# Row sums of the softmax taken in four 64x64 blocks of TensorE instead of four 128x32 strips, and a first quad whose keys are transposed unnormalised, in a fused attention and SoLU block

## The chip, the cores and the metric

The kernel runs on one core of a Trainium2 chip. The metric is the device time of one execution in microseconds (us). Three executions of the kernel before took 782.05, 782.74 and 783.13 us, so the median is 782.74 us. Engines have the names of the profile: PE is TensorE (PEld its weight loads), DVE is VectorE, ACT is ScalarE, POOL is GpSimd, and SP is SyncE, which issues most of the DMAs; SPq, ACTq and POOLq are the queues of instructions of those engines.

## What is computed

```python
# attention: q, k, v are (8, 12, 448, 64) float32
rmsnorm(x, g) = x / sqrt(mean(x * x, axis=-1) + 1e-6) * g
q_n, k_n = rmsnorm(q, g_q), rmsnorm(k, g_k)
scores = q_n @ k_n.T / sqrt(64)
attn = exp(scores - max(scores))
attn = attn / (sum(attn) + 1e-9)
x = (attn @ v) laid out as (3584, 768)
# SoLU block: w_in (768, 1024), w_out (1024, 768), float64 as given
h = x @ w_in
u = h * softmax(h)
out = layernorm(u) * g_ln @ w_out
```

The kernel does not subtract the maximum of the scores: the normalised rows and the gains bound them, and a second, general path takes over where they do not. That path does not run on these inputs.

## The kernel before

The 96 heads are worked on in 24 groups of four, called quads; a quad is two pairs of heads, `i` = 0, 1 numbers the pair and `h` = 0, 1 the head in it. Everything on PE is float32, and each matmul of the program stands in the trace as two MATMUL records, since float32 is done in two parts.

**A quad of the steady state (quads 1 to 23).** The 448 keys of a head are 7 blocks of 64. For each block, `both_scores` (line 870, matmul in L879) multiplies keys by queries of all four heads: four matmuls of 64 rows by 64 columns by 448 queries, each in another quarter of the PE array, which therefore run at the same time. I call four such matmuls a set; a set is 8 records. ACT takes the exponentials of the set's 128x896 result in one instruction (L839). `both_values` (line 884, L891) multiplies the exponentials by v, again one set for each block. So a quad is 14 sets. The score tiles stand in PSUM buffers with the tag `t`, of which there are three.

**The sums of the softmax.** DVE adds some of a quad's seven tiles of exponentials together first (`add_pair`, `add_to`), so that 4 tiles are left for each of quads 1 and 2, and 3 for each of quads 3 to 23. What is left is called the terms. `sums` (line 941, L951) adds each term's partitions on PE with a matrix of ones, for one quad, then two, then three quads at a time (`sums_at`, line 1458: after quads 2, 5, 8 and so on to 23; quad 0 has its own). A term takes four matmuls: all 128 partitions, 32 columns of ones, and a quarter of the 896 columns, 224, each, in four column strips of the array. ACT copies the result (`keep_sums`, line 957, at most two copies), and a DMA stores it for a later stage that divides by it.

```python
sm[g : g + 32, j % 2, j // 2 * S // 2 : (j // 2 + 1) * S // 2], ones[:, w], e[:, h, t * S // 2 : (t + 1) * S // 2],
```

**Quad 0, the start.** Nothing can be prefetched for it, so it has functions of its own. `load_rows` brings q and k of its two pairs in rows (112 partitions of four rows), through SP's queue (q) and ACT's (k). For pair 0, DVE and ACT square q and k, DVE sums the squares (`sum_rows`, L783), ACT starts the reciprocal root (`rsqrt_seed`, L713 and L714) and DVE improves it (`rsqrt_step`, L720 to L723), DVE multiplies (`normalise_rows`, L802), PE transposes (L809), and ACT copies the transposed q and k out of PSUM (`take_rows`, L817 and L819). The gains of q and k come as one column through POOL, DVE, PE and ACT (`gain_column`). Then come three score tiles of pair 0 (L849), one tile of the last 64 keys of all four heads (`scores_last`, L862), three of pair 1, the values (L925, and L936 with 128 rows by 64 columns, two matmuls at a time), and the sums of 5 terms: three of pair 0's tiles were added by DVE (`add`, L910) and POOL (`add_more`, L914). Before all this PE runs five matmuls on zeros (`warm_up`, L793).

The order of all instructions is written out by hand (`tc.manual_schedule`, from line 1492); each engine takes its own in that order. After the attention come the products with w_in (L1103) and w_out (L1329) on PE.

Of the kernel before, what the change touches and what calls it, by code (L numbers as in the profile page):

```python
# [366 lines left out]
def fast_path(  # L367
# [58 lines left out]
    ones = work.tile([P, 3, 32], FP32, tag="ones", name="ones", bufs=1)  # L426
# [22 lines left out]
    def setup():  # L449
        nc.gpsimd.memset(mhalf, -0.5)  # L450
        nc.gpsimd.memset(seven, 7.0)
        nc.gpsimd.memset(eps, 1e-6)


        for i, x in enumerate((-1.9375, -1.00390625, -(0.1249 ** 2))):
            nc.gpsimd.memset(limits[:, i : i + 1], x)


        nc.gpsimd.memset(ones, 0.0)
        for i in range(2):  # L460
            c = slice(16 * i, 16 * i + 16)
            nc.gpsimd.memset(ones[:, i, c], 1.0)
            nc.gpsimd.memset(ones[i * D : (i + 1) * D, 2, c], 1.0)
        make_identity(nc, ident)
# [17 lines left out]
    def gain_column():  # L482
# [10 lines left out]
        pg = ps_t.tile([P, KF], FP32, tag="t", name="pg")[:, 0:1]  # L493
        nc.tensor.transpose(pg, gg[:, 2:4].rearrange("o h d -> o (h d)"), ident[0:1, 0:1])
        nc.scalar.copy(gcol[:, KF : KF + 1], pg)
# [181 lines left out]
    def squares_half(n, s, vector):  # L677
# [4 lines left out]
        if vector:  # L682
            nc.vector.tensor_tensor(y, x, x, OP.mult)
        else:
            nc.scalar.activation(y, x, AF.Square)
# [61 lines left out]
    def qk_transpose(n):  # L747
        d = st[n]
        turned(n)
        nc.vector.transpose(d["qkT"].rearrange("p s t -> p (s t)"), d["qkn"].rearrange("p b d -> p (b d)"))  # L750
# [8 lines left out]
    def load_rows(n, queues):  # L759
        b, hp = divmod(n, NP)  # L760
        d = st[n] = {}
        d["qk"] = xs.tile([P, 2, 2, 4, D], FP32, tag="x", name="x")[0:R]
        for s, src in enumerate((q, k)):
            for h in range(2):
                queues[2 * s + h].dma_start(
                    d["qk"][:, s, h], src[b, 4 * (hp // 2) + hp % 2 + 2 * h].rearrange("(p j) d -> p j d", p=R)
                )

    def square_rows(n, s, engine):
        d = st[n]  # L770
        if s == 0:
            d["sq"] = xs.tile([P, 2, 2, 4, D], FP32, tag="x", name="xsq")[0:R]
        x, y = d["qk"][:, s], d["sq"][:, s]
        if engine is nc.scalar:
            nc.scalar.activation(y, x, AF.Square)
        else:
            engine.tensor_tensor(y, x, x, OP.mult)

    def sum_rows(n, s):
        d = st[n]  # L780
        if s == 0:
            d["ss"] = work.tile([P, 4 * NB], FP32, tag="ss", name="ss", bufs=2)[0:R, 0:16]
        nc.vector.tensor_reduce(  # L783
            d["ss"][:, s * 8 : s * 8 + 8], d["sq"][:, s].rearrange("p h j d -> p (h j) d"), AX, OP.add
        )

    def warm_up():

        w = work.tile([P, 2, S], FP32, tag="el", name="warm", bufs=3)[:, 0]
        nc.vector.memset(w, 0.0)  # L790
        o = ps_t.tile([P, 2, 512], FP32, tag="o", name="pt", bufs=1)[:, 0, 0:S]
        for _ in range(5):
# [5 lines left out]
    def normalise_rows(n, s):  # L798
        d = st[n]
        y = d["y"][:, s * 8 : s * 8 + 8].rearrange("p (h j) -> p h j ()", h=2).to_broadcast([R, 2, 4, D])  # L800
        o = flat(d["sq"][:, s]).rearrange("p (j h d) -> p h j d", h=2, d=D)
        nc.vector.tensor_tensor(o, d["qk"][:, s], y, OP.mult)  # L802

    def transpose_rows(n, s):
        d = st[n]
        pt = ps_t.tile([P, 2, 512], FP32, tag="o" if n and s == 0 else "t", name="pt", bufs=1 if n and s == 0 else 3)
        d["pt", s] = pt[:, 0, 0:S]
        for j in range(4):
            nc.tensor.transpose(  # L809
                d["pt", s].rearrange("p (r j) -> p j r", j=4)[:, j], flat(d["sq"][:, s])[:, j * P : (j + 1) * P], ident[0:R, 0:R]  # L810
            )

    def take_rows(n, s):
        d = st[n]
        if s == 0:
            turned(n)
# [1100 lines left out]
```

## Time and profile before

| what | value |
| --- | --- |
| three executions | 782.05, 782.74, 783.13 us |
| the profiled execution: its time / its span (first to last instruction) | 781.84 us / 780.0 us |
| granted TensorE clock, mean | 0.998 |
| PE busy | 771.0 us, 5262 instructions |
| DVE, ACT, POOL busy | 603.6, 508.9, 487.3 us |
| DMA moved | 134.27 MB, mean 172 GB/s |

The profile is one execution. Its page gives each engine's busy time, the span in 40 slices, the chain of work that ended last, and the costliest groups of instructions; other views of the same trace list the waits of an engine, the chain in order of time, and the instructions of an engine in order of time. In such a row the first number is the start, the second the time taken, both in us; a group of instructions is merged into one row with its count (x8 is 8 records), and brackets hold the idle time ahead of it and what ended it. Matmul records are pipelined, so the time of one record (0.54 us for 448 columns) is longer than what it costs in a stream; the cost is read from the distance between starts, which the chain's rows give.

### The profile page before, as it was taken

What the parts mean: (1) busy time and instruction counts of PE and PEld (TensorE: products, weight loads), DVE (VectorE), ACT (ScalarE), POOL (GpSimd) and SP (SyncE); (2) the same over time, 40 slices, a digit from 0 to 9 for tenths busy, and PEclk for the clock granted to TensorE, in tenths of its full rate; (3) what the DMA queues carried; (4) which work ended last, traced back from release to release, by engine and by line L of the source; (5) the groups of instructions that cost most, each with busy time, mean ns of one, the idle gap of its engine ahead of it and who ended that gap; (6) DMA issues with size and microseconds to landing.
All of it is one profiled execution on the core that took longest, in us unless ns stands there. A gap on an engine that the chain in (4) does not pass through costs nothing.

```text
span 780.0 us, 15087 instructions
## 1 busy us (share of the span) xinstructions
PE 771.0 (99%) x5262; PEld 478.3 (61%) x5262; DVE 603.6 (77%) x1064; ACT 508.9 (65%) x833; POOL 487.3 (62%) x635
## 2 busy tenths in 40 slices
PE   8999999999999999999999999999999999999997
PEld 4444445445454444444444444444899999999996
DVE  6878999999999983687777667685797695776844
ACT  6778898888989862787777656655626445464510
POOL 2565444455464552455687688888898787777862
PEclk9999999999999999999999999999999999999999
DMA  9999999999999367588887777773757647456312
GB/s 164 173 188 192 194 198 176 200 209 187 186 203 172 91 171 165 130 196 182 195 203 169 161 150 165 163 182 69 224 154 240 207 145 256 144 188 242 104 62 87
DMA packets 279818, 134.27 MB, mean 172 GB/s; under 512 B 190324, under 2 KB 264884, under 8 KB 279732
## 3 DMA queue, kind: packets, MB, share of 16 engines
q1 hardware_dynamic: 265892, 123.31, 70.4%
q10 hardware_dynamic: 13840, 9.90, 4.4%
q8 instruction: 44, 0.72, 0.4%
q14 instruction: 42, 0.34, 0.1%
HBM read 96.12 MB, written 37.04 MB: 171 GB/s over the span
## 4 chain that ended last, share of the span: by engine, by line
PE 94%; SPq 3%; DMA 1%; DVE 0%; POOL 0%; ACT 0%; issue 0%; POOLq 0%; ACTq 0%
PE A L1329 16%; PE o L891 15%; PE s L879 15%; PE A L1103 14%; PE B L1103 9%; PE B L1329 8%; PE D L1103 5%; PE C L1103 5%; PE C L1329 4%; PE sm L951 4%; SPq L647 2%; DMA qk<-in_k_dram 0%; DMA gg<-in_g_q_dram 0%; DVE part L696 0%; POOL ss L706 0%
## 5 line engine op out<-in xcount | busy, mean ns | idle before, releaser
L879 PE MATMUL s<-qkT 64*64 64x448 f32 x1288 | 139.3, 540 | 0.3 <-ACT qkT L745 0.2
L839 ACT ACTIVATE E<-s 128x896 f32<-128x896 f32 x144 | 124.5, 920 | 20.5 <-PE s L879 19.7
L729 POOL TENSOR_TENSOR qkn<-qk,ny 128x896 f32<-128x896 f32 x45 | 77.2, 1736 | 72.9 <-DVE ny L723 33.5
L891 PE MATMUL o<-E,v 64*64 64x448 f32 x1104 | 120.4, 536 | 0.0
L879 PEld LDWEIGHTS s<-qkT 64*64 64x64 f32 x1288 | 66.1, 191 | 60.0 <-issue 38.8
L1329 PE MATMUL A<-w_out,sums 128*128 128x192 f32 x392 | 79.8, 326 | 0.0
L1329 PE MATMUL B<-w_out,sums 128*128 128x192 f32 x392 | 79.8, 326 | 0.0
L891 PEld LDWEIGHTS o<-E,v 64*64 64x64 f32 x1104 | 42.4, 133 | 56.2 <-issue 49.0
L1103 PE MATMUL A<-w_in,xg 128*128 128x512 f32 x168 | 76.8, 593 | 0.0
L1103 PE MATMUL B<-w_in,xsum 128*128 128x512 f32 x168 | 76.7, 592 | 0.0
L1329 PEld LDWEIGHTS B<-w_out,sums 128*128 128x128 f32 x392 | 66.4, 190 | 0.0
L1329 PEld LDWEIGHTS A<-w_out,sums 128*128 128x128 f32 x392 | 66.4, 190 | 0.0
L750 DVE STREAM_TRANSPOSE qkT<-qkn 128x896 f32<-128x896 f32 x46 | 49.9, 1098 | 9.4 <-POOL qkn L729 9.4
L1103 PEld LDWEIGHTS B<-w_in,xsum 128*128 128x128 f32 x168 | 31.9, 190 | 40.2 <-issue 39.9
L1103 PEld LDWEIGHTS A<-w_in,xg 128*128 128x128 f32 x168 | 31.8, 190 | 40.1 <-issue 38.4
L905 DVE TENSOR_TENSOR es<-es,E 128x896 f32<-128x896 f32 x44 | 49.3, 1120 | 4.4
L1205 ACT ACTIVATE u<-u,shift,he 128x1024 f32<-128x1024 f32 x28 | 34.8, 1241 | 27.2 <-POOL shift L1201 27.1
L696 DVE TENSOR_REDUCE part<-sq 128x28 f32<-128x896 f32 x46 | 47.9, 1074 | 4.3 <-ACT sq L690 4.3
L1079 POOL TENSOR_TENSOR xsum<-xg 128x384 f32<-128x384 f32 x14 | 14.4, 1030 | 57.2 <-ACT xsum L1062 35.0
L899 DVE TENSOR_TENSOR es<-E 128x896 f32<-128x896 f32 x46 | 50.1, 1089 | 0.0
L1329 PE MATMUL A<-w_out,s 128*128 128x192 f32 x224 | 45.6, 326 | 0.0
L690 ACT ACTIVATE sq<-qk 128x896 f32<-128x896 f32 x45 | 41.0, 944 | 2.1 <-DMA qk<-in_k_dram 0.7
(173 smaller groups left out, 1655.4 us busy)
## 6 DMA issues: line engine op xcount, KB each, us to landing
ur<-ud SPq DMA_DIRECT2D x60, 256.0 KB, 4.7
ud<-ub SPq DMA_DIRECT2D x112, 128.0 KB, 2.8
xd<-xo SPq DMA_DIRECT2D x48, 224.0 KB, 4.2
qk<-in_q_dram SPq DMA_DIRECT2D x92, 112.0 KB, 4.2
qk<-in_k_dram SPq DMA_DIRECT2D x92, 112.0 KB, 4.0
v<-in_v_dram SPq DMA_DIRECT2D x23, 448.0 KB, 5.2
out_dram<-P SPq DMA_DIRECT2D x19, 384.0 KB, 4.0
raw<-in_moe_w_in_dram SPq DMA_DIRECT2D x12, 512.0 KB, 5.0
```

The lines of the kernel that those rows point to most:

```text
L690: nc.scalar.activation(d["sq"].rearrange("p (s b) d -> p s (b d)", s=2), d["qk"], AF.Square)
L696: nc.vector.tensor_reduce(norms[m]["part"][:, i], st[n]["sq"], AX, OP.add)
L729: e.tensor_tensor(d["qkn"].rearrange("p (s b) d -> p s b d", s=2), d["qk"].rearrange("p s (b d) -> p s b d", d=32), y.rearrange("p (s b) - ...
L750: nc.vector.transpose(d["qkT"].rearrange("p s t -> p (s t)"), d["qkn"].rearrange("p b d -> p (b d)"))
L839: nc.scalar.activation(e, s[:, :, 0:S], AF.Exp)
L879: nc.tensor.matmul(s[i * D : (i + 1) * D, h, 0:S], qkT[hh, i, 1, keys], qkT[hh, i, 0], start=True, stop=True)
L891: nc.tensor.matmul(d["o"][h * D : (h + 1) * D, i, 0:S], d["v"][pp, h, kc], d["E", kc][pp, h], start=kc == 0, stop=kc == NK - 1,)
L899: nc.vector.tensor_tensor(e, d["E", x], d["E", y], OP.add)
L905: engine.tensor_tensor(e, e, d["E", x], OP.add)
L1103: nc.tensor.matmul(k[bank], a[:, c], w_in[i][:, c], start=begin and c == 0, stop=c == HD - 1, skip_group_check=not begin,)
L1205: nc.scalar.activation(d["u"], d["u"], AF.Identity, scale=d["e"], bias=d["shift"])
L1329: nc.tensor.matmul(k[bank], a[:, c].rearrange("p a i -> p (a i)"), w_out[:, area, i, c], start=begin and c == 0, stop=c == KC - 1, skip_gr ...
```

## The change

It has three parts.

**Sums of all quads.** A term's sum is taken as `both_values` takes the values: 64 partitions (one pair's half of the keys), 64 columns of ones, all 448 queries of a head, in four quarters of the array. The matrix of ones becomes a window into a row of 112 columns, shifted by 16 for each quad, so that up to three quads add into the same 448 columns of PSUM. Quad 0 has all its exponentials summed by PE: the additions by DVE and POOL go, and its terms are 7 instead of 5; six of them hold one pair and take two matmuls of 128 rows by 64 columns. `keep_sums` is one copy of 128x896, and two DMAs store it.

**Quad 0's keys.** k is loaded with its rows spread so that three transposes of 128x128 turn it as loaded, before its norms are known. The reciprocal norms of the keys enter as the per-partition `scale` of the exponentials, one head at a time, so each 128x896 exponential of quad 0 becomes two of 128x448.

**Order of the start.** q of pair 0 goes first, one half on SP's queue and one on ACT's, then q of pair 1; k of pair 0 follows on both; k of pair 1 and the last 64 keys go through POOL's queue in four DMAs. The steps of pair 0's q alone run ahead of the other norms. Warming takes four matmuls. The squares of quad 1's q move from DVE and ACT to POOL, and its transposes on DVE are split.

On PE from the start to the scores of the last keys of quad 0, where `pt` and `pk` are transposes, `pg` is the gain column, `s` scores (L849 and L893 of one pair, L862 and L907 of the last keys), and `warm` the zeros, there stood:

```order
L793 MATMUL pt<-warm 128x448 x5
L494 MATMUL pg<-ident,gg 128x1
L809 MATMUL pt<-ident,xsq 128x112 x8
L849 MATMUL s<-qkT 64x448 x12
L809 MATMUL pt<-ident,xsq 128x112 x8
L862 MATMUL s<-qkT 64x448 x4
L849 MATMUL s<-qkT 64x448 x12
```

In the changed kernel PE has, over the same stretch:

```order
L819 MATMUL pt<-warm 128x448 x3
L851 MATMUL pk<-ident,x 128x128 x3
L819 MATMUL pt<-warm 128x448
L491 MATMUL pg<-ident,gg 128x1
L834 MATMUL pt<-ident,xsq 128x112 x4
L893 MATMUL s<-qkT 64x448 x4
L851 MATMUL pk<-ident,x 128x128 x3
L855 MATMUL pk<-ident,x 128x128
L893 MATMUL s<-qkT 64x448 x4
L834 MATMUL pt<-ident,xsq 128x112 x4
L893 MATMUL s<-qkT 64x448 x4
L907 MATMUL s<-qkT 64x448 x4
```

Four transposes of normalised q are left between the gain column and the first scores, where eight of q and k stood; those of pair 0's k stand ahead of the gain column, and pair 1's transposes stand between the score tiles of pair 0. Further on, quad 0's sums are 16 matmuls of 448 columns where 20 of 224 stood.

On PE at the end of quad 2, with the sums of quads 1 and 2 (`sm`; `El`, `es` and `E` are terms), between the last values (`o`) and the first scores of quad 3, there stood:

```order
L891 MATMUL o<-El,v 64x448 x4
L951 MATMUL sm<-El,ones 32x224 x4
L951 MATMUL sm<-es,ones 32x224 x8
L951 MATMUL sm<-E,ones 32x224 x4
L951 MATMUL sm<-El,ones 32x224 x4
L951 MATMUL sm<-es,ones 32x224 x8
L951 MATMUL sm<-E,ones 32x224 x4
L479 MATMUL pg<-ident,grow 128x8
L879 MATMUL s<-qkT 64x448 x16
```

and now stand:

```order
L937 MATMUL o<-El,v 64x448 x4
L995 MATMUL sm<-El,ones 64x448 x4
L995 MATMUL sm<-es,ones 64x448 x8
L995 MATMUL sm<-E,ones 64x448 x4
L995 MATMUL sm<-El,ones 64x448 x4
L995 MATMUL sm<-es,ones 64x448 x8
L995 MATMUL sm<-E,ones 64x448 x4
L476 MATMUL pg<-ident,grow 128x8
L925 MATMUL s<-qkT 64x448 x16
```

The number and order of the matmuls are as before; each sum writes 64 partitions by 448 columns where it wrote 32 by 224.

On POOL at the start, from the filling of the ones or of the identity (`ident`) on, there stood:

```order
L459 MEMSET ones 128x96
masks.py:197 MEMSET ident 128x128
L462 MEMSET ones 128x16
L463 MEMSET ones 64x16
L462 MEMSET ones 128x16
L463 MEMSET ones 64x16
masks.py:199 ISA
masks.py:199 AFFINE_SELECT ident<-ident 128x128
L486 TENSOR_TENSOR gg<-gg 1x64
L488 TENSOR_SCALAR large<-gmax 1x1
L914 TENSOR_TENSOR es<-es,E 128x896
```

and now stand:

```order
masks.py:197 MEMSET ident 128x128
L460 MEMSET ones 128x16
L774 DMA x<-in_k_dram 128x3x64
masks.py:199 ISA
masks.py:199 AFFINE_SELECT ident<-ident 128x128
L774 DMA x<-in_k_dram 128x3x64
L777 DMA x<-in_k_dram 64x2x64 x2
L1531 MEMSET ss 128x14
L483 TENSOR_TENSOR gg<-gg 1x64
L485 TENSOR_SCALAR large<-gmax 1x1
L684 TENSOR_TENSOR sq<-qk 128x448
```

Four DMA issues and a memset stand ahead of the product of the two gains (`gg`), and the identity, which PE's transposes need, stands behind the first of those DMAs.

The core of the diff:

```diff
@@ load_rows
+            for h, queue in enumerate((nc.sync, nc.scalar)):
+                queue.dma_start(dst[:, h], pairs(q, n)[h].rearrange("(p j) d -> p j d", p=R))
+        load_gains()
+        setup()
+        for n, queues in enumerate(((nc.scalar, nc.sync), (nc.gpsimd, nc.gpsimd))):
+            dst = flat(st[n]["qk"][:, 1]).rearrange("p (j h d) -> p h j d", h=2, d=D)
             for h in range(2):
+                queues[h].dma_start(dst[:, h, 0:NJ], pairs(k, n)[h, 0 : NJ * P].rearrange("(p j) d -> p j d", j=NJ))
+        dst = flat(st[0]["qk"][:, 1]).rearrange("p (j h d) -> p j h d", h=2, d=D)[:, NJ]
+        for n in range(2):
+            nc.gpsimd.dma_start(dst[n * D : (n + 1) * D], pairs(k, n)[:, NJ * P : S].rearrange("h p d -> p h d"))
@@ exponentials
-        nc.scalar.activation(e, s[:, :, 0:S], AF.Exp)
+        for h, y in enumerate(norm):
+            nc.scalar.activation(e[:, h], s[:, h, 0:S], AF.Exp, scale=y)
+        if not norm:
+            nc.scalar.activation(e, s[:, :, 0:S], AF.Exp)
@@ sums
         for j, m in enumerate(ms):
-            terms = quads[m]["terms"]
-            for x, (w, e) in enumerate(terms):
+            w = ones[:, 48 - 16 * j : 112 - 16 * j]
+            for pair, e in quads[m]["terms"]:
                 for h in range(2):
-                    for t in range(2):
-                        g = 32 * (2 * h + t)
-                        nc.tensor.matmul(
-                            sm[g : g + 32, j % 2, j // 2 * S // 2 : (j // 2 + 1) * S // 2], ones[:, w], e[:, h, t * S // 2 : (t + 1) * S // 2],
-                            start=(x == 0), stop=(x == len(terms) - 1),
-                        )
+                    if pair < 2:
+                        runs.append((h, pair, w, e[:, h]))
+                        continue
+                    for i in range(2):
+                        pp = slice(i * D, (i + 1) * D)
+                        runs.append((h, i, w[pp], e[pp, h]))
+        for x, (h, i, w, e) in enumerate(runs):
+            same = [y for y, r in enumerate(runs) if r[:2] == (h, i)]
+            nc.tensor.matmul(sm[h * D : (h + 1) * D, i, 0:S], w, e, start=x == same[0], stop=x == same[-1])
@@ keep_sums
-        nc.scalar.copy(r[:, 0:w], sm[:, 0:w, 0 : S // 2])
-        if n == 3:
-            nc.scalar.copy(r[:, 2], sm[:, 0, S // 2 : S])
+        nc.scalar.copy(r, sm[:, :, 0:S])
@@ the start
+        square_rows(0, True)
+        square_rows(1, False)
+        sum_rows(0)
+        rsqrt_seed(rn[0])
+        transpose_keys(0)
+        square_keys(0)
+        warm_up(1)
         gain_column()
+        rsqrt_step(rn[0])
+        take_keys(0)
+        take_gain()
+        normalise_rows(0)
+        transpose_rows(0)
+        take_rows(0)
+        sum_rows(1)
+        sum_keys(0)
+        rsqrt_seed(rn[1])
+        rsqrt_step(rn[1])
...
-        add(0)
-        add_more(0)
...
-        quads[0]["terms"] += [(0, st[0]["es"])] + [(1, st[1]["E", x]) for x in range(NJ)]
+        quads[0]["terms"] = [(n, st[n]["E", x]) for n in range(2) for x in range(NJ)]
+        quads[0]["terms"] += [(2, quads[0]["E", NJ])]
```

214 lines of the change are left out of this document (113 added, 101 removed).

## Prediction

> **What bounds the kernel now.** I read the page first: how busy the engines are, and the share of each in the chain that ended last.
>
> ```profile
> PE 771.0 (99%) x5262; PEld 478.3 (61%) x5262; DVE 603.6 (77%) x1064; ACT 508.9 (65%) x833; POOL 487.3 (62%) x635
> PE 94%; SPq 3%; DMA 1%; DVE 0%; POOL 0%; ACT 0%; issue 0%; POOLq 0%; ACTq 0%
> ```
>
> PE is busy for 771.0 of 780.0 us, and the chain is PE's own stream of matmuls. Being busy alone does not prove it, since a matmul's end is modelled, so the next view is the list of all waits of PE:
>
> ```profile
> PE pt L793 <- DVE warm L790: 1.4, 1, 1.4
> PE pt L809 <- DVE xsq L802: 1.0, 1, 1.0
> PE s L849 <- ACT qkT L819: 0.6, 1, 0.6
> PE s L879 <- ACT qkT L745: 0.2, 1, 0.2
> ```
>
> Three of the four waits lie in the start. Whatever the change adds to PE's stream from quad 1 on has only 0.2 us of waiting to hide in. So the first question is what a set of matmuls costs in a stream, and the chain in order of time answers it; here two quads and a group of sums (start, time, records):
>
> ```profile
> 72.13 3.01 PE s L879 x32
> 75.14 0.75 PE o L891 x8
> ...
> 77.39 0.86 PE s L879 x8
> ...
> 79.76 3.01 PE o L891 x32
> 82.76 3.54 PE sm L951 x72
> 86.31 3.23 PE s L879 x32
> ```
>
> A set of four 64x64 matmuls over 448 columns (8 records) takes 0.75 us, 3.01 for four, whether scores or values. The 72 records of sums are nine terms in 3.54 us, 0.39 each: a strip of 224 columns takes about half as long as a quarter's 448. No gap stands between the rows. Last, the groups of instructions with their shapes tell how many sums there are:
>
> ```profile
> L891 PE MATMUL o<-E,v 64*64 64x448 f32 x1104 | 120.4, 536 | 0.0
> L951 PE MATMUL sm<-es,ones 128*32 128x224 f32 x376 | 22.2, 352 | 0.0
> L951 PE MATMUL sm<-El,ones 128*32 128x224 f32 x192 | 13.7, 357 | 0.0
> L951 PE MATMUL sm<-E,ones 128*32 128x224 f32 x40 | 2.4, 352 | 0.0
> ```
>
> 376 + 192 + 40 = 608 records, at 8 to a term, are 76 terms: 5 of quad 0, 8 of quads 1 and 2, 63 of quads 3 to 23.
>
> **The sums, quads 1 to 23.** The number of matmuls stays (four to a term), but each streams 448 columns instead of 224, in the shape, the quarters and the PSUM banks of `both_values`. So a term becomes a set, and I price it by the rows of L891: 3.01 / 4 = 0.7525 us. The halves of the array are no gain here: a strip of 128 rows sums the keys of both pairs at once, a quarter only those of one, so twice the columns pass.
>
> A group of three quads goes from 3.54 to 9 x 0.7525 = 6.77, so +3.23. The row behind it (86.31) shows four sets of scores in 3.23 instead of 3.01: 0.22 us for the first matmuls behind a group of another shape. In the changed kernel sums and scores have one shape, and I take the 0.22 as gone: +3.01 for each of the six groups that scores follow. The seventh ends the attention and has w_in's product behind it:
>
> ```profile
> 295.00 0.59 PE L951 MATMUL sm<-El,ones 128*32 128x224 f32 x8
> ...
> 298.54 2.84 PE L1103 MATMUL A<-w_in,xg 128*128 128x512 f32 x6
> ```
>
> There it is 298.54 - 295.00 = 3.54 to 6.77, +3.23. For quads 1 and 2 a transpose of the gains stands between sums and scores:
>
> ```profile
> 47.32 3.16 PE sm L951 x64
> 50.49 0.15 PE pg L479
> 50.64 3.23 PE s L879 x32
> ```
>
> so the 0.22 stays with it, and eight terms go from 3.16 to 6.02: +2.86. Together 6 x 3.01 + 3.23 + 2.86 = 24.2 us.
>
> The Trainium skill (TensorEngine Tiling (Array Packing), Tiling Modes, Key Properties) has the rule that changing the tiling mode, not just the tile, drains TensorE. The trace agrees so far: 3.23 against 3.01. By this rule alone the change would gain its 0.22 us six times; by the columns it loses ten times that.
>
> The other end: if the 0.22 belongs to any group of sums (their weights, their PSUM buffer), it stays six times, 1.3 us, and so may 0.12 us at each group's entry (nine terms take 3.54, eight 3.16 in the row at 47.32 below, so one more term costs 0.38 and nine 3.42; for nine groups 1.1 us). That makes 26.6 instead of 24.2. On the low side, one set in a quad takes 0.86 instead of 0.75 (row 77.39); if that is a wait for an ACT that the longer sums let catch up, 23 x 0.11 = 2.5 us come back. I take neither: the 0.86 also stands in a quad that has no sums ahead of it.
>
> ACT's two copies of a group's sums become one of 128x896, and the store one DMA more; ACT has 14% of slack, and the copy is over long before the third score tile needs the buffer:
>
> ```profile
> 118.10:154.00 35.90, 35.90 (x424) 17.62 (x428) 33.32 (x47) 31.12 (x44) 15.88 (x23) 1.00 1.03 193
> ```
>
> These are PE, PEld, DVE and ACT busy in 35.90 us: ACT 31.12. Cost nothing.
>
> **The sums of quad 0.** PE in order of time, at the start:
>
> ```profile
> 10.23 2.52 PE L849 MATMUL s<-qkT 64*64 64x448 f32 x24 [0.62 <-ACT qkT L819]
> 18.38 4.73 PE L936 MATMUL o<-E,v 128*64 128x448 f32 x24
> 23.04 0.59 PE L951 MATMUL sm<-El,ones 128*32 128x224 f32 x8
> 25.07 3.30 PE L879 MATMUL s<-qkT 64*64 64x448 f32 x32
> ```
>
> Five terms take 25.07 - 23.04 = 2.03 us, and the scores behind them 3.30, 0.29 over 3.01. Now six terms take two matmuls of 128x64 each, just as L936's twelve, which take 23.04 - 18.38 = 4.66, and one is a set: 4.66 + 0.75 = 5.41. So 5.41 - 2.03 - 0.29 = +3.1 us. Dropping `add` and `add_more` frees DVE and POOL, which nobody waits for here. The longer sums also cover quad 1's preparation, which before was ready only just in time.
>
> All sums: 24.2 + 3.1 = **+27.3 us**, 29.7 at the other end (24.2 becoming 26.6).
>
> **The start.** DVE, ACT and POOL, in order of time:
>
> ```profile
> 4.17 0.69 DVE L777 TENSOR_TENSOR xsq<-x 112x512 f32<-112x512 f32 x1 [2.85 <-DMA x<-in_q_dram]
> 4.90 1.28 DVE L783 TENSOR_REDUCE ss<-xsq 112x8 f32<-112x512 f32 x2
> 7.48 1.15 ACT L775 ACTIVATE xsq<-x 112x512 f32<-112x512 f32 x2
> 9.64 0.53 ACT L819 COPY qkT<-pt 128x448 f32<-128x448 f32 x1
> 11.31 2.54 ACT L839 ACTIVATE E<-s 128x896 f32<-128x896 f32 x3 [0.65 <-PE s L849]
> 14.23 0.97 ACT L690 ACTIVATE sq<-qk 128x896 f32<-128x896 f32 x1
> 15.54 0.94 ACT L839 ACTIVATE El<-s 128x896 f32<-128x896 f32 x1
> 19.61 0.90 ACT L839 ACTIVATE E<-s 128x896 f32<-128x896 f32 x1
> 4.75 0.31 POOL L486 TENSOR_TENSOR gg<-gg 1x64 f32<-1x64 f32 x1 [2.84 <-DMA gg<-in_g_k_dram]
> ```
>
> On the path to the first scores (10.23), one of two sums of squares goes (1.28 / 2 = 0.64) and the copy of k behind that of q (0.53): first scores 1.17 us earlier, if q lands as now. It may land up to 0.4 earlier, as its second half no longer stands behind the first on SP's queue:
>
> ```profile
> 0.72 0.40 SPq L765
> 1.19 0.41 SPq L765
> ```
>
> Of the 1.17, ACT gives some back. Seven exponentials of 2.54 / 3 = 0.85 become fourteen of half a tile, at most 1.15 / 2 = 0.58 each by L775: +0.3 a tile. The scores wait for the exponentials to free PSUM, so up to the fourth tile (El, now ending at 15.54 + 0.94 = 16.48) that is +1.2, and a seed of some 0.5 is added, while the 0.97 of L690 and more of quad 1's squares leave ACT: net some 0.3 later. The last exponential (ending at 20.51) is needed only by the last pair of values, 0.78 before 23.04, at 22.26; that 1.7 us of slack and the earlier start hold the rest. The start: 1.17 - 0.3 = **-0.9 us**; ends -1.6 (q early, nothing given back) and, by POOL below, above zero. The spared warming matmul runs while PE would wait for the rows: nothing.
>
> **The sum.** 27.3 - 0.9 = +26.4. The profiled execution took 781.84 us (span 780.0 and 1.84 around it), so 808.2; the median of the three runs is 0.90 above it, so I forecast **809.1 us**.
>
> **Rivals.** *POOL holds up the start.* Four DMA issues now stand ahead of `gg`'s product on POOL, and DVE's gain steps, ahead of the norm's last step, wait for it. POOL had 2.84 us idle there, so it decides from 0.71 us an issue on; the trace has no DMA of POOL's. The nearest rows are SP's issues, up to 1.00 us, and POOL's own long work, 2.10:
>
> ```profile
> 5.82 1.00 SPq L647
> 15.47 2.10 POOL L914 TENSOR_TENSOR es<-es,E 128x896 f32<-128x896 f32 x1 [8.88 <-DVE es L910]
> ```
>
> At 1.00 four take 4.0, 1.2 more than the idle time, and the start gains nothing; at 2.10 they take 8.4, 5.6 more, and it loses 4.4. At 1.5 it is 6.0 - 2.84 - 1.17 = 2.0 lost: 782.74 + 27.3 + 2.0 = 812.0. I take under 0.71, as SP's first issues take near 0.4.
>
> The Trainium skill (SBUF — State Buffer, SBUF: two separate sides) warns against DMAs issued from GpSimd: a VectorE operation in a 2-port mode locks GpSimd out while it writes descriptors. No run here shows it; DVE idles for 2.85 us ahead of 4.17, when these issues would fall. The page has one such DMA at about 620 ns alone and 3100 ns under the lock; four of these would make an estimated 12.4 us, 9.6 beyond the idle time, and about 818.
>
> *The cost between groups stays*: 782.74 + 29.7 - 0.9 = 811.5. *The quarters don't run at once* in the sums, because each matmul waits for its neighbour's bank or weights: two at a time would take 1.5 us a set and add 72 x 0.75 = 54 us more (71 sets, and quad 0's one): 863. L879 and L891 speak against it, in the same quarters.
>
> *The sums are hidden, so it is not slower.* The attention could be paced by something else, with PE's rows only seeming full: the DMA share in the window above is 1.03, and DVE is busy for 33.32 of 35.90. If a group of sums were followed by 3 us in which PE would wait for DVE or loads anyway, the sums would cost nothing and only the start would show: 782.74 - 0.9 = 781.8. It decides if 27 us of waits lie between 25.07 and 298.54; PE's list has 0.2 us, and sets follow at 0.75 without a gap. Very unlikely.
>
> **How the numbers follow.** Forecast 0.62; POOL late 0.20; cost between groups stays 0.10; quarters not at once 0.04; hidden 0.03; 0.01 for the rest. The range: low 782.05 (the fastest run) + 27.3 - 1.6 - 2.5 = 805.2; high, late POOL at some 1.9 us an issue, 813.5; I give 805.0 to 813.5. A measurement of this kernel can tell about 0.2%, 1.6 us. Slower by more: 0.97; within: 0.02; faster: 0.01, both from the hidden case.
>
> **What would show it.** L995's rows should merge at 0.75 us for 8 records, nine terms in 6.77, and the scores behind them in 3.01, not 3.23. The first scores should start near 9.1, quad 1's near 27.5 (25.07 + 5.41 - 2.03 - 0.9), and w_in's product near 325. PE's list of waits should stay as short. From there to the end nothing should differ. I am wrong if sums take 0.4 us a term, if rows of PE idle appear behind them, or if the start is off by over 2 us.

## The result, and the profile after

The changed kernel took **810.9 us**, the median of 5 runs (810.58 to 811.47), beside 782.74 for the kernel before (5 runs, 782.04 to 783.21): a ratio of 1.0365, 95% interval 1.035 to 1.0379. The change makes the kernel 3.65% slower. The profiled execution took 810.9 us, its span 809.1. In two of the experiments below (split sends and sums first) one execution each, of 1638.69 and 1375.2 us, ran in a slow state and is in no ratio.

First, how busy the engines are in the changed kernel, and its chain by engine:

```profile
PE 797.5 (99%) x5251; PEld 482.4 (60%) x5251; DVE 603.1 (75%) x1069; ACT 511.1 (63%) x834; POOL 486.5 (60%) x638
PE 94%; SPq 2%; DMA 1%; DVE 1%; ACT 0%; POOL 0%; issue 0%; POOLq 0%; ACTq 0%
```

PE's busy time rose by 26.5 us, from 771.0, and the others' hardly moved (DVE 603.6 to 603.1, ACT 508.9 to 511.1, POOL 487.3 to 486.5). PE was the bound and got more to do. All its waits:

```profile
PE pt L819 <- DVE warm L815: 1.4, 1, 1.4
PE s L893 <- ACT El L881: 1.3, 1, 1.3
PE s L893 <- ACT qkT L843: 0.8, 1, 0.8
PE pk L851 <- DMA x<-in_k_dram: 0.3, 1, 0.3
PE s L925 <- ACT qkT L744: 0.3, 1, 0.3
```

The list has five rows where there were four, and 3.8 of its 4.1 us lie in the start. New are the second row, a score tile that waits for ACT to have read another, and the fourth, the first transposes of k, which wait for k to land. Now the sums, in the chain of the changed kernel in order of time (start, time, records):

```profile
50.78 6.01 PE sm L995 x64
...
56.94 3.23 PE s L925 x32
...
86.05 3.01 PE o L937 x32
89.06 6.76 PE sm L995 x72
95.82 3.01 PE s L925 x32
```

Nine terms take 6.76 us, 0.751 each, just as a set of scores or values, and eight take 6.01. The scores behind nine terms take 3.01, no longer 3.23; behind the transpose of the gains (at 56.94) they still take 3.23. The groups with their shapes show that every quarter of a term streams 448 columns:

```profile
L995 PE MATMUL sm<-es,ones 64*64 64x448 f32 x368 | 38.7, 536 | 0.0
L995 PE MATMUL sm<-El,ones 64*64 64x448 f32 x192 | 22.4, 537 | 0.0
L995 PE MATMUL sm<-E,ones 128*64 128x448 f32 x24 | 4.7, 539 | 0.0
```

The last of these is quad 0, with two matmuls to a term. PE in order of time, at the start, at the end of the attention and at the end:

```profile
6.45 0.52 PE L851 MATMUL pk<-ident,x 128*128 128x128 f32 x3 [0.33 <-DMA x<-in_k_dram]
...
7.93 0.60 PE L834 MATMUL pt<-ident,xsq 112*128 112x112 f32 x4
9.32 1.01 PE L893 MATMUL s<-qkT 64*64 64x448 f32 x8 [0.78 <-ACT qkT L843]
...
16.91 1.01 PE L893 MATMUL s<-qkT 64*64 64x448 f32 x8 [1.26 <-ACT El L881]
...
23.17 4.68 PE L995 MATMUL sm<-E,ones 128*64 128x448 f32 x24
...
28.58 3.19 PE L925 MATMUL s<-qkT 64*64 64x448 f32 x32
...
325.76 2.84 PE L1143 MATMUL A<-w_in,xg 128*128 128x512 f32 x6
...
800.86 0.81 PE L1369 MATMUL B<-w_out,sums 128*128 128x192 f32 x4
```

The last row stood before as

```profile
773.63 0.81 PE L1329 MATMUL B<-w_out,sums 128*128 128x192 f32 x4
```

From these rows, and the same ones before, follows where the time went. "Last product" is the start of the last record of PE's last product by w_out, 0.49 us behind that of its group of four.

| mark, us from the start of the span | before | after | difference |
|---|---|---|---|
| first scores | 10.23 | 9.32 | -0.91 |
| sums of quad 0 | 23.04 | 23.17 | +0.13 |
| first scores of quad 1 | 25.07 | 28.58 | +3.51 |
| first product by w_in | 298.54 | 325.76 | +27.22 |
| last product | 774.12 | 801.35 | +27.23 |
| end of the span | 780.03 | 809.11 | +29.08 |

The sums cost 27.22 - 0.13 = 27.1 us. The start is 0.9 earlier at the first scores and 0.1 later at the end of the first quad. In the 475.6 us of the SoLU block nothing changed. Behind the last product the span is 29.08 - 27.23 = 1.85 us longer, which the prediction did not have.

One trace of each kernel is compared here, and such rows scatter. Two kernels further down (the two in which POOL merges terms) have the program of before up to quad 3, yet 24.9 and 25.0 us lie between the starts of their first two groups of sums, where 24.2 lie before: PE waits 1.0 us for quad 1's transposed rows in them, 0.2 before. So a difference of some tenths in this table means little, and from median to median the loss is 28.2 us, not 29.1.

### The profile page after: what moved, and what is told of

It reads as the page before. It is cut to its first block, busy times and chain, and to the rows that moved or that the text cites. A ratio compares the mean times of both kernels' runs of the same rounds, so it can differ in the third digit from the quotient of the medians.

```text
span 809.1 us, 15095 instructions
## 1 busy us (share of the span) xinstructions
PE 797.5 (99%) x5251; PEld 482.4 (60%) x5251; DVE 603.1 (75%) x1069; ACT 511.1 (63%) x834; POOL 486.5 (60%) x638
## 4 chain that ended last, share of the span: by engine, by line
PE 94%; SPq 2%; DMA 1%; DVE 1%; ACT 0%; POOL 0%; issue 0%; POOLq 0%; ACTq 0%
PE A L1369 16%; PE o L937 14%; PE s L925 14%; PE A L1143 13%; PE B L1143 9%; PE B L1369 8%; PE sm L995 7%; PE C L1143 4%; PE D L1143 4%; PE C L1369 4%; SPq L646 1%; DVE part L695 1%; DMA qk<-in_q_dram 0%; DMA xd<-xo 0%; DMA gg<-in_g_q_dram 0%
## 5 line engine op out<-in xcount | busy, mean ns | idle before, releaser
L883 ACT ACTIVATE E<-s 128x896 f32<-128x896 f32 x138 | 119.3, 922 | 18.3 <-PE s L925 18.3
L1245 ACT ACTIVATE u<-u,shift,he 128x1024 f32<-128x1024 f32 x28 | 34.8, 1241 | 28.2 <-POOL shift L1241 28.1
L1222 DVE CUSTOM_DVE_ANT_0 u<-h,u 128x1024 f32<-128x1024 f32 x28 | 38.7, 1380 | 3.9 <-ACT u L1214 3.9
```

The lines of the kernel that those rows point to most:

```text
L883: nc.scalar.activation(e, s[:, :, 0:S], AF.Exp)
L1222: nc.vector.tensor_tensor_reduce(u, h, u, 1.0, 0.0, OP.mult, OP.add, total)
```

## The experiments

Ratios are to the kernel before on the same chip, whose median was 782.0 to 782.5 in each set.

**The two halves alone.** The first kernel is the changed one with the sums of before (`ones` and its memsets, `sums`, `keep_sums`, and the view of `rd`); the second is the kernel before with those of the change. Of the first one's edit, the matmul in `sums`:

```diff
-            nc.tensor.matmul(sm[h * D : (h + 1) * D, i, 0:S], w, e, start=x == same[0], stop=x == same[-1])
+                        nc.tensor.matmul(
+                            sm[g : g + 32, j % 2, j // 2 * S // 2 : (j // 2 + 1) * S // 2], ones[:, w], e[:, h, t * S // 2 : (t + 1) * S // 2],
+                            start=(x == 0), stop=(x == len(terms) - 1),
+                        )
```

> The changed kernel with the sums of before (four strips of 128x32 by 224 columns a term); quad 0 keeps its 7 terms. My theory, that the sums' columns on PE are the whole loss and the start gives nothing: quads 1 to 23 cost what they did before, quad 0's sums take 7 x 0.39 = 2.8 us instead of 2.0, the start is 0.1 later, so PE's last product is about 0.9 us later than before, and the time is 783.7, or 784.5 if what follows the last product is about 0.9 us longer because POOL now issues DMAs. Rival, that the start's reordering or its DMAs cost a large part through the attention: 790 or more. Rival, that the start does gain its forecast 0.9: 782.6.

> The kernel before with only the sums of the change (four quarters of 64x64 by 448 columns a term); quad 0 has its 5 old terms, four of them pairs'. My theory: quads 1 to 23 add 23.7 us as the trace of after shows between quad 1's first scores and w_in's first product, quad 0 goes from 2.03 to 4 x 0.78 + 0.75 = 3.9, so 782.7 + 23.7 + 1.8 = 808.2. Rival, that the new start shares the loss: under 800.

The new start with the old sums took 783.61 us (ratio 1.0026, interval 1.0016 to 1.0037), the old start with the new sums 809.11 (1.0344, 1.0328 to 1.036). So the sums are nearly all of the loss, and the new start gains nothing. PE of the first kernel around the sums of quad 0:

```profile
23.84 2.48 PE L991 MATMUL sm<-E,ones 128*32 128x224 f32 x48
26.63 3.30 PE L928 MATMUL s<-qkT 64*64 64x448 f32 x32
```

With strips, the new start's seven terms take 26.63 - 23.84 = 2.79 us and the scores behind them 3.30: with this start alone quad 1 begins 1.6 later than before (25.07). One half of that is the start's (23.84 for 23.04), the other the two terms more (2.79 for 2.03), which DVE and POOL added up before. The start's half goes with k: its transposes began at 7.04 in this trace and at 6.45 in the changed kernel's, and what follows on PE moved with them (first scores at 9.90 and 9.32). Which of the two is the usual one, single traces do not show.

**Columns or shape?** A term may be dear because its quarters stream 448 columns, or because quarters are slower than strips at this. Here the quarters stay and stream half the columns; the sums of the second half of the queries are left out, and ACT copies the first half's result twice in their place:

```diff
-            nc.tensor.matmul(sm[h * D : (h + 1) * D, i, 0:S], w, e, start=x == same[0], stop=x == same[-1])
+            nc.tensor.matmul(sm[h * D : (h + 1) * D, i, 0 : S // 2], w, e[:, 0 : S // 2], start=x == same[0], stop=x == same[-1])
```

> The changed kernel with each sum taken over 224 of the 448 columns alone: the second half of the queries is left out of the sums and is divided by the first half's. My theory, that a set costs by the columns that it streams: a term costs 0.376 us instead of 0.752, nine terms 3.4, scores behind them in 3.01, so 810.9 - 71 x 0.376 - (6 x 0.39 + 0.376) = 781.5. Rival, that the 64x64 shape itself (half the rows, so two matmuls for one) costs: 795 or more.

It took 784.68 us (1.0032, 1.0021 to 1.0043). Its chain in order of time:

```profile
84.19 3.40 PE sm L995 x72
87.59 3.01 PE s L925 x32
```

Nine terms take 3.40 us: a quarter with 224 columns costs what a strip with 224 costs (3.54 with its change of shape). So the price goes by the columns streamed, and the strips' advantage is that one column passes 128 keys' rows instead of 64. The time is 3 us above what I expected, though. In the trace the span is 3.1 us longer than before: 0.8 by the start, 0.8 by quad 0's sums, 1.8 behind the last product, and only -0.3 in quads 1 to 23, where 0.14 in each of six groups and 0.22 behind them should have given 2.2. New waits of PE took most of that back:

```profile
PE o L937 <- DVE xo L1030: 0.8, 2, 0.5
PE o L937 <- ACT El L883: 0.8, 1, 0.8
```

**What a change of shape costs.** Into each group of sums of three quads I put eight matmuls of one column, behind every set but the last: in one kernel in the shape of a strip, in the other in that of the quarters around it.

```diff
+            if len(ms) == 3 and x % 4 == 3 and x + 1 < len(runs):
+                nc.tensor.matmul(sm[0:32, 0, 511:512], ones[:, 0:32], ident[:, 0:1], start=False, stop=False, skip_group_check=True)
```

The second kernel has `sm[0:64, 0, 511:512], ones[0:64, 0:64], ident[0:64, 0:1]` there.

> The changed kernel with one matmul of 128x32 over a single column behind every fourth sum of a three-quad group (8 in a group, 56 in all), written to a PSUM column that nobody reads. If a change of the array's shape costs, as the 0.22 us behind a group and some 0.14 at its entry suggest, each insertion costs about 0.36 plus a little for itself: a group of 72 records goes from 6.76 to about 9.8, and the time from 810.9 to about 832. Rival, that the 0.22 came from the group's weights or buffer and not from the shape: as the 64x64 insertion, a group of 7.3 or less and 814 or less.

> The control of the run beside it: the same 56 insertions as 64x64 matmuls over a single column, so the array keeps its shape. Both theories: only the cost of a small matmul itself, 0.02 to 0.07 us each, 811 to 815.

They took 827.89 and 822.33 us (one run each); I had expected 832, and 811 to 815. PE in order of time, first with strips and then with quarters put in:

```profile
88.89 0.93 PE L995 MATMUL sm<-El,ones 64*64 64x448 f32 x8
89.75 0.22 PE L997 MATMUL sm<-ident,ones 128*32 128x1 f32 x2
89.91 0.98 PE L995 MATMUL sm<-es,ones 64*64 64x448 f32 x8
...
98.16 2.06 PE L925 MATMUL s<-qkT 64*64 64x448 f32 x20
```

```profile
93.63 0.93 PE L995 MATMUL sm<-El,ones 64*64 64x448 f32 x8
...
101.27 2.10 PE L925 MATMUL s<-qkT 64*64 64x448 f32 x20
```

A group takes 98.16 - 88.89 = 9.27 and 101.27 - 93.63 = 7.64 instead of 6.76 us: 0.31 and 0.11 for each matmul put in. The difference, 0.20 us, is what two changes of shape cost, less than the 0.36 that I had expected; the quarter put in costs more than its 0.02 to 0.07. One thing is not separated: the strip lies across two quarters of the array, the quarter put in takes one, so part of the 0.20 may be a longer wait for the matmuls that still run there. That the 0.22 behind each group before belonged to the shape rests on more than this: it is gone in the kernel with half the columns too (3.01 behind 3.40), whose sums have the columns of before and the shape of the change. The whole times can't be compared: the second kernel started late, for another reason (the last section).

**POOL's DMAs.** Here k's four DMAs leave POOL's queue for ACT's and SP's:

```diff
-        for n, queues in enumerate(((nc.scalar, nc.sync), (nc.gpsimd, nc.gpsimd))):
+        for n, queues in enumerate(((nc.scalar, nc.sync), (nc.scalar, nc.sync))):
...
-            nc.gpsimd.dma_start(dst[n * D : (n + 1) * D], pairs(k, n)[:, NJ * P : S].rearrange("h p d -> p h d"))
+            (nc.scalar, nc.sync)[n].dma_start(dst[n * D : (n + 1) * D], pairs(k, n)[:, NJ * P : S].rearrange("h p d -> p h d"))
```

> The changed kernel with the four DMAs of POOL issued by ACT and SP. If the 1.9 us that the profiled execution lost behind PE's last product comes from POOL's queue being used at all, this stretch is as before (5.9 us from the start of PE's last matmul of w_out to the end of the span) and the time is 809 to 810. If it is scatter of the end, the time is 810.5 to 811.5. In the start, the product of the gains stands ready earlier (0.3 us less waiting on DVE); with pair 1's keys landing later, quad 0's sums start within 0.7 us of 23.2.

It took 810.6 us (1.0371, 1.0356 to 1.0385), the same as the change; quad 0's sums start at 22.98 instead of 23.17. So with the issues on the other queues the start is 0.2 us earlier: POOL's hold it up by little. POOL of the changed kernel shows why:

```profile
1.50 1.01 POOL L774 DMA_DIRECT2D x<-in_k_dram  x1 [0.21 <-issue]
...
2.87 0.78 POOL L774 DMA_DIRECT2D x<-in_k_dram  x1
3.65 1.22 POOL L777 DMA_DIRECT2D x<-in_k_dram  x2
...
4.91 0.31 POOL L483 TENSOR_TENSOR gg<-gg 1x64 f32<-1x64 f32 x1
```

The four take 3.01 us, 0.75 each, a little over the 0.71 from which they delay anything; `gg` starts at 4.91, where it started at 4.75. The stretch behind the last product stayed at 7.65, so POOL's DMAs are not the cause of that either.

**The longer end.** In the first of these two kernels, the kernel before stores each group's sums in two DMAs on SP's queue instead of one; in the second, the changed kernel issues one of its two from ACT's queue.

```diff
-            nc.sync.dma_start(sd[ms[0] : ms[0] + n].rearrange("j r c -> r j c"), r[0:P:16, 0:n])
+            for c in (slice(0, S // 4), slice(S // 4, S // 2)):
+                nc.sync.dma_start(sd[ms[0] : ms[0] + n].rearrange("j r c -> r j c")[:, :, c], r[0:P:16, 0:n, c])
```

```diff
-                nc.sync.dma_start(rows[h], r[h * D : h * D + 16 * n : 16].rearrange("j i t -> j (i t)"))
+                (nc.sync, nc.scalar)[h].dma_start(rows[h], r[h * D : h * D + 16 * n : 16].rearrange("j i t -> j (i t)"))
```

> The kernel before with each store of sums split into two DMAs on SP, as the change has them, and nothing else. PE's work is that of before. If the longer end (5.9 us from PE's last matmul of w_out to the end of the span before, 7.3 to 7.8 in the runs with the new sums) comes from SP's longer program, which puts a stall of its instruction fetch between the last waits, then the end is 7.2 or more here too and the time 783.0 to 784. Rival, that it has to do with the sums themselves or is scatter: 5.9 to 6.3, and 781.6 to 782.6.

> The changed kernel with one edit: of the two DMAs that store each group's sums, the second is issued from ACT's queue instead of SP's. So nine DMA issues leave SP, as many DMAs and bytes run as before the edit, and PE's program is the same. In the trace of the changed kernel 7.76 us lie behind the start of the last product's last matmul, 5.92 before the change and 7.49 in the old kernel with each store split in two on SP's queue. Theory (the longer end belongs to the number of SP's own instructions): the stretch falls to 5.9 to 6.3 us, the span by some 1.6 from 809.1 to about 807.5, and the time from 810.9 to about 809.3. Rival (it belongs to the stores themselves, to the layout they write or to the longer run of the whole program): the stretch stays at 7.2 to 7.8 and the time at 810.9, or above if ACT's nine issues of 0.4 us show between groups. PE's sums stay at 6.77 a group and the way from w_in's first product to the last matmul at 475.6 in either case.

The kernel before with split stores took 783.91 us (1.002, 1.0011 to 1.003), with 7.49 us behind the last product instead of 5.92. The changed kernel with stores on ACT took 816.18 (1.0429, 1.0414 to 1.0443), with 6.63 instead of 7.76. The second missed both of my expectations. Its stretch shrank, but not to the 5.9 to 6.3 of the theory, and its time rose by 5.3: 5.7 us are lost between quad 0's sums and w_in's first product (below), 1.1 come back at the end, and the traced execution started 2.2 us late (last section).

Where the stretch grows can be seen in the trace's record of SP's own instructions. The program ends with a list of waits for semaphores on SP, one every 0.06 to 0.09 us, and a few last steps in which the engines wait for each other. In most kernels there is a stall in it, always at the same place in SP's program, between the 903rd and the 904th of its instructions in the trace. The stall in the table is the time between their starts.

| kernel | instructions on SP | stall, us | behind the last product, us |
|---|---|---|---|
| before; POOL merges; POOL merges later | 902 | none | 5.92; 5.75; 7.24 |
| new start with old sums; scores first; sums first; stores on ACT | 905 | 0.62; 0.53; 0.95; 0.84 | 6.25; 6.15; 6.85; 6.63 |
| split sends; old start with new sums | 911 | 1.22; 1.24 | 7.49; 7.27 |
| no POOL DMA | 912 | 1.56 | 7.65 |
| after; half columns; strips put in; quarters put in | 914 | 1.40; 1.55; 1.24; 1.22 | 7.76; 7.77; 7.20; 7.22 |

In all eleven kernels that have a 904th instruction on SP it starts 5.8 to 6.6 us behind the last product, whatever PE does, and what is left of the list comes behind it: 0.3 us in kernels of 905 instructions, 1.3 us in those of 914. Split sends changes nothing but SP's DMAs of the kernel before, and it has the stall; moving nine issues off SP shortens the changed kernel's from 1.40 to 0.84. So the length of SP's program decides, and not the stores or their layout, which are the same in the changed kernel and in stores on ACT. That SP waits there for the next piece of its program is an inference: a DMA of the kind "instruction" lands near there, but also in kernels without a stall. The stall is 1.4 of the 1.85 us. (POOL merges later, with 7.24, has no 903rd instruction on SP, and SP's last stands at 5.89; there PE's own last instruction comes 1.3 us behind all the others.)

The second kernel also shows what the cheap place in ACT was worth. Its chain in order of time, behind a group of sums:

```profile
92.59 6.81 PE sm L995 x72
...
99.42 0.92 ACT r L1003
...
100.36 0.69 ACTq L1008
...
101.09 0.93 ACT E L883
...
102.06 1.04 PE s L925 x8
```

One DMA issue of 0.69 us between ACT's copy and its first exponential (I had counted on 0.4) puts ACT on the chain, and 32.30 instead of 31.57 us lie between groups, 0.73 more. The copy itself is free there; the next 0.7 us are not.

**The start alone.** In two kernels with the new start and the old sums, the order of the start is changed. In the first all three score tiles of pair 0 stand ahead of pair 1's transposes; in the second quad 0's norms of pair 1's keys are summed earlier as well:

```diff
-        transpose_keys(1)
-        take_keys(1)
...
+        unit(lambda: scores(0, 2))
...
+        transpose_keys(1)
+        take_keys(1)
...
-        unit(lambda: scores(0, 2))
```

```diff
+        sum_keys(1)
+        sum_keys(1, True)
...
-        sum_keys(1)
-        sum_keys(1, True)
```

> The changed start with the sums of before, and the three score tiles of pair 0 ahead of pair 1's transposes on PE and on DVE. In the changed start ACT waited for score tiles for 0.35, 0.32 and 0.18 us between quad 0's exponentials, because PE's transposes of pair 1 stood between them. If that is where the start's gain went, quad 0's sums start 0.7 to 0.85 us earlier, relative to the first scores, than in the changed kernel (13.85 us behind them there, 13.0 to 13.2 here), and the time is 0.7 to 0.85 below the 783.6 of the run with the changed start and the old sums. Rival, that ACT's doubled exponentials bound it alone: no difference, 13.8 behind the first scores.

> The run with the scores of pair 0 first, where ACT no longer waited for PE but 0.77 and 0.29 us for DVE's sums of pair 1's squares and the step behind them; now these sums stand ahead of pair 1's transposes in DVE's order. If the start's gain goes from one wait of ACT to the next, this takes away both: quad 0's sums start about 0.9 us earlier behind the first scores than in that run (14.04 there, 13.1 here), and the time is 0.9 below its 783.7. Rival, that ACT's fourteen half exponentials fill the time alone: 14.0, no difference.

They took 783.71 us (1.0024, 1.0014 to 1.0034) and 784.14 (1.0019, 1.001 to 1.0029): neither differs from the new start as it is (783.61), where I had expected 0.7 to 0.85 less of the first and 0.9 less of the second. My theory for the first, that ACT waits for scores, falls. ACT in order of time, in the changed kernel and then in the first of these:

```profile
10.43 1.16 ACT L881 ACTIVATE E<-s,ny 128x448 f32<-128x448 f32 x2
11.93 1.16 ACT L881 ACTIVATE E<-s,ny 128x448 f32<-128x448 f32 x2 [0.35 <-PE s L893]
13.41 1.16 ACT L881 ACTIVATE E<-s,ny 128x448 f32<-128x448 f32 x2 [0.32 <-PE s L893]
...
15.70 1.16 ACT L881 ACTIVATE El<-s,ny 128x448 f32<-128x448 f32 x2 [0.18 <-PE s L893]
```

```profile
14.70 0.30 ACT L715 ACTIVATE ny<-ss,eps 128x8 f32<-128x8 f32 x1 [0.77 <-DVE ss L811]
...
16.04 1.16 ACT L884 ACTIVATE El<-s,ny 128x448 f32<-128x448 f32 x2 [0.29 <-DVE ny L725]
```

The waits for PE went, and waits for DVE's norms came in their place (0.77 and 0.29): the first scores to the sums of quad 0 took 14.04 us, 13.85 in the changed kernel. With the norms summed earlier they took 13.46, so those waits were real, though worth less than the 0.9 that I expected of them; and the 0.4 us did not arrive at the end: from quad 0's sums to the next group 25.74 us pass instead of the 24.98 of the new start as it is, a stretch that scatters. That ACT's fourteen half exponentials fill most of the time is then the likely rest, but no run here takes them away.

**Fewer terms.** If PE's columns are the price, a term less should gain. In the kernel before, POOL adds one term of each quad from 3 on to another, at once in the first kernel, later in the second:

```diff
+                    e4 = quads[m]["terms"].pop()[1]
+                    e0 = quads[m]["terms"][0][1]
+                    nc.gpsimd.tensor_tensor(e0, e0, e4, OP.add)
```

```diff
+                    if m > 3 and m - 1 not in sums_at:
+                        t = quads[m - 1]["terms"]
+                        nc.gpsimd.tensor_tensor(t[1][1], t[1][1], t[2][1], OP.add)
+                        t.pop()
```

> The kernel before, with the sums' columns cut instead of doubled: in quads 3 to 23 POOL adds the second of the three terms to the first, so that PE sums two terms, six for a group instead of nine. If PE's columns are what counts, in both directions, each of 21 terms returns 0.38 us, 8 us in all: 774. Rival, that DVE, ACT or POOL take over as soon as PE is faster, as the waits for DVE and ACT in the run with half the columns hint: 779 or more, with PE waits behind the groups of sums.

> The kernel before with 14 of the 63 terms of quads 3 to 23 merged by POOL, but of a quad that is not the last of its group, and in the next quad, behind that quad's products on POOL; in the run with all 21 merged POOL waited 68 us in total for DVE's tiles, with the next quad's products queued behind. If that wait was what lost 33 us, and PE's columns otherwise decide, a group has seven terms instead of nine and the time falls by 14 x 0.38 = 5.3 us to 777. Rival, that POOL's product of two tiles itself is too much for POOL or slows DVE: 782 or more, with waits of PE for the transposed rows.

They took 815.64 us (1.0426, 1.0412 to 1.044) and 794.47 (1.0152, 1.0138 to 1.0165): both lose. In the first, POOL stands waiting for DVE with the next quad's product queued behind it (the waits of POOL):

```profile
POOL es L1698 <- DVE es L899: 67.8, 18, 4.6
```

and PE waits 22.2 us in seven groups for the terms that POOL adds.

In the second that wait is gone, and seven terms take 2.79 us on PE as they should; but between groups 33.0 to 34.6 us pass instead of 31.79. The waits of PE and of ACT, and POOL's copies of the row sums, in the second kernel:

```profile
PE s L879 <- ACT E L839: 11.2, 6, 2.5
```

```profile
ACT ny L713 <- POOL ss L707: 32.1, 15, 3.2
```

```profile
L706 POOL COPY ss<-part 32x56 f32<-32x56 f32 x92 | 64.1, 696 | 13.4 <-DVE part L696 9.4
```

The four small copies with which POOL gathers a quad's row sums take 696 ns each instead of 274, and they stand behind POOL's product of two terms, 2.17 us each. ACT, in whose order the norms' first step stands ahead of exponentials, waits 32.1 us for these sums, where no such wait is among its nine longest before; its exponentials come late, and PE waits for them. (DVE's sums beside it take 1259 ns instead of 1089.) Why the copies are slower is open. Columns added to PE cost their full time; columns taken from it gain nothing when POOL has to pay for them.

## Why the prediction was right, and where it was not

*The bound.* PE's stream from quad 1 on had nothing to hide in. Right: the half with the new sums alone is 27 us slower, and the rival that the sums are hidden is out.

*The sums of quads 1 to 23.* Priced as sets, 0.7525 us a term; measured 0.751. Nine terms 6.76 against 6.77, and 3.01 for the scores behind. That columns are the reason is shown by the kernel with half of them.

*The 0.22 us behind a group.* It went in all six places and stayed behind the gains' transpose. The matmuls put in show a price of a changed shape of that size (0.20 for two changes). So far the trace agrees with the rule of the Trainium skill (TensorEngine Tiling (Array Packing), Tiling Modes, Key Properties) that a change of mode drains TensorE. The rival that the cost between groups stays is out; likewise that quarters do not run at once. The prediction put the loss by columns at ten times this gain; by its own terms it is near twenty times (24.2 + 1.3 against 1.3).

*The sums of quad 0.* 5.41 us forecast, 5.41 measured. All sums: +27.3 forecast, +27.1 measured.

*The start.* This step failed: -0.9 forecast, +0.13 measured, inside the ends that I gave. Two terms of it were wrong.

The first is the 1.17 us at the first scores, of which 0.91 came, although q landed 0.6 earlier (the squares start at 3.56 instead of 4.17). I had followed q alone. On PE the transposes of k, a warming matmul and the gain's column stand ahead of q's transposes, and they wait for k to land. DVE has q's rows ready at 6.74 + 0.69 = 7.43:

```profile
6.74 0.69 DVE L828 TENSOR_TENSOR xsq<-x,ny 112x512 f32<-112x512 f32 x1
```

PE transposes them at 7.93. In the four traces with this start in which these matmuls run at full speed, k's transposes start at 6.45, 6.46, 6.70 and 7.04, and the first scores come 2.86 to 2.87 us behind them each time. So half a microsecond of the gain stood behind k here, and a whole one where k's transposes began at 7.04 (q's rows ready at 7.52, transposed at 8.52).

The second is what comes behind the first scores. I had 0.3 us for it, and 13.85 - 12.81 = 1.04 us came. From the first exponential to the fourth tile's end (El) 16.86 - 10.43 = 6.43 us pass instead of 16.48 - 11.31 = 5.17, so 1.3. Of this, 4 x 0.3 for two exponentials of half a tile instead of one was in the sum, but so was a saving by squares that leave ACT, and ACT's waits for PE's tiles (0.35, 0.32 and 0.18 above) were not; PE then waits 1.26 for ACT ahead of its last tile. POOL's issues were 0.75 us each, at the edge that I named. The Trainium skill's warning (SBUF — State Buffer, SBUF: two separate sides), with 3100 ns for a DMA issued from GpSimd under the lock, did not come true here: the longest took 1.01 us. DVE stood idle until 3.56, though, so the trace hardly puts it to the test.

*"From there to the end nothing should differ."* This step failed. From w_in's first product to the last product it holds, 475.58 us in both kernels; behind it come 1.85 us, of which 1.4 are a stall in SP's last instructions. I had put the doubled stores at nothing as DMAs that are hidden, and had not counted them as instructions of SP's program.

*The sum.* 26.4 us were forecast from profile to profile and 29.1 came: 1.0 too little for the start, 1.85 for the end, 0.2 too much for the sums. The 0.9 that I added to come to the median hid a third of that, 809.1 against 810.9, and that was luck: the changed kernel's profiled execution was itself the median.

## What to carry to other kernels

Price a reduction by matmul with ones by the columns that pass, not by the number of matmuls: a strip that takes all 128 rows needs half the columns of two quarters of 64, and in a kernel bound by PE those columns are paid one for one, while a change of array shape costs about a tenth of a microsecond. Before an engine is called slack, look at what stands next in its queue at that place: 0.7 us behind ACT's free copy cost 0.73. And count instructions on a queue as well as bytes.

## What the runs showed of the hardware that was not expected

**SP's program and the end.** Eleven of fourteen kernels stall at the same place in SP's program, behind its 903rd instruction, for 0.5 to 1.6 us; the three whose program on SP ends before it do not (the table above). Why exactly there is open.

**A matmul rate that comes late.** The kernel with quarters put in, in its one traced execution, ran the start's matmuls at about half speed; PE in order of time:

```profile
6.91 0.88 PE L851 MATMUL pk<-ident,x 128*128 128x128 f32 x3 [0.69 <-DMA x<-in_k_dram]
7.58 1.70 PE L819 MATMUL pt<-warm 128*128 128x448 f32 x2
...
11.32 1.77 PE L893 MATMUL s<-qkT 64*64 64x448 f32 x8 [0.79 <-ACT qkT L843]
```

The same scores took 1.01 us in the changed kernel, from 9.32 on, and here full speed came only near 17.5: quad 0's sums began at 27.91, 4.7 later. The granted clock of the windows reads 1.00 all the while, so it does not show this; the rows do. The kernel with stores on ACT ran its warming and first transposes as slowly up to about 10.6 (quad 0's sums at 25.32). In both, k had come some 0.5 us later than in the changed kernel (6.91 and 7.00 for 6.45) while the warming still ran slowly; but half columns and sums first, with k at 6.80 and 6.84, were at full speed by 7.5. The Trainium skill (TensorE: Matmul & The Clock Gate, Part 1: The HAM clock gate (the "warmup" mystery)) has TensorE slow until it has been busy for one of the windows that run on by themselves, so that the moment differs from run to run; the rows agree, and a warming that is split by a wait for a DMA, as this change has it, seems to leave it to chance. In the kernel without POOL's DMAs k came in time (6.01), nothing split the warming, and full speed was there by 6.6; one trace does not show that this always holds.
